# Score matmuls in four row groups of 32 instead of two of 64, with banks always filled by three and re-planned costs

## The chip, the cores and the metric

One core of one Trainium2 chip. The metric is device time in microseconds (us) of one execution, lower is better. Engines: PE is TensorE, ACT is ScalarE, DVE is VectorE. Times below are medians of several executions.

## The reference, cut to what matters

Two layers, each a multi-query attention block and then a linear-attention block, on x of 2048 x 512. In attention 32 heads of size 16 share one K and one V.

```python
q = (x @ wq)            # 2048 x 32 heads x 16
k = x @ wk              # 2048 x 16, shared by all heads
v = x @ wv
scores = einsum("bhqd,bkd->bhqk", q, k) * 16 ** -0.5
p = softmax(scores)     # 2 layers x 32 heads x 2048 x 2048 exponentials
o = einsum("bhqk,bkd->bhqd", p, v)
```

Cut into tiles of 128 keys x 512 queries, there are 4096 score tiles in the two layers. Every one needs a score matmul, an exponential of 128 x 512 values, and a matmul with V ("PV").

## The kernel before

A scheduler inside the kernel simulates the engines with planned costs and fixes, at build time, in which order each engine gets its instructions. On the chip only semaphores decide when they start. So a planned cost is never executed, but it shapes the order.

Score tiles go two ways. ACT takes two or three PSUM banks at a time ("a fill") and computes exp on 1024 or 1536 columns. DVE takes tiles through bank 6 and computes exp by arithmetic, in pairs ("DVE score tiles"). The kernel uses eight PSUM banks: 0 to 2 and 3 to 5 are ACT's two sets, 6 serves DVE's scores and all other work (projections, transposes), 7 collects PV.

```python
    RG = 64                                  # rows of the array per score matmul
    NRG, NM = P // RG, RG // DH              # 2 row groups, 4 masked copies of K
    FILL, FILLW, FILLN = 0.6, 1.7, 512       # aim for PE's streaming share
    SHARE = True                             # bank 5 may be lent to other work
    ...
    def tdv(n, c=1.04): return 0.065 + n * c * 1e-3    # planned cost on DVE
    def tac(n):         return 0.09 + n * 0.833e-3     # planned cost on ACT
    ...
        # one fill: a score matmul per bank, row group i of head i
        def smm(self, e, ps_, b0):
            for k, p in enumerate(ps_):
                ...
                r = slice(i * RG, (i + 1) * RG)
                x = e.matmul(bank(b0 + k), lhsT=Kr[r, m, kt * P:(kt + 1) * P],
                             rhs=QT[r, ...], start=True, stop=True)
    ...
            for s in (0, 1):                 # the two sets of banks
                w = 3
                if s == 1 and SHARE and (not banks.free[5] or (not banks.free[6] and self.waiting())):
                    w = 2                    # second set without bank 5
    ...
    def idle(now):                           # PE has nothing to do: zero matmul into bank 7
        if not sc.order[PE] or streaming(now) > FILL * FILLW:
            return
        ...
        o = add(PE, ..., lambda e: e.matmul(bank(7, FILLN), lhsT=zer[:], rhs=maskx[:].bitcast(BF16)[:, 0:FILLN], ...), name="dummy")
```

A head's 16 rows are picked from the row group by a copy of K in which the other rows are zero: RG / 16 copies.

The softmax here doesn't subtract the row's maximum and nothing guards it: scores larger than these inputs give would overflow.

## Time and profile before

| | before |
|---|---|
| time (three executions) | 1849.07 us (1846.9 to 1851.51) |
| exps on ACT | 1039 of 1536 columns, 227 of 1024 |
| DVE score tiles | 523 |
| zero matmuls | 594 |

From the profile's page: the busy line (busy us, share of the span, instructions), the chain that ended last, and four groups (line, engine, operation, out<-in, shapes, count, busy us, mean ns of one, idle time just before them and what ended it).

```profile
PE 1754.5 (95%) x11002; PEld 515.1 (28%) x11002; DVE 1658.7 (90%) x2966; ACT 1739.9 (94%) x1529; POOL 34.2 (2%) x46
...
PE 44%; DVE 43%; ACT 11%; issue 1%; POOL 1%; DMA 0%; SPq 0%
...
L775 ACT ACTIVATE PTA<-ps_all 128x1536 bf16<-128x1536 f32 (+1 forms) x1268 | 1640.6, 1398 | 59.4 <-PE ps_all L635 52.1
L635 PE MATMUL ps_all<-QT,Kr 64*128 64x512 bf16 x4096 | 835.1, 383 | 42.0 <-DVE xT L829 16.0
...
L829 DVE TENSOR_SCALAR xT<-ps_all 128x512 int32<-128x512 f32 x523 | 358.8, 686 | 48.9 <-PE ps_all L635 45.7
...
L897 PE MATMUL ps_all<-maskx,zer 128*128 128x512 bf16 x594 | 205.0, 387 | 0.0
```

Three engines are at 90% or more. L775 is ACT's exp, L635 the score matmul, L897 the zero matmul, L829 DVE's first step on a score tile. The timeline of PE (start us, us, what) shows two fills:

```profile
441.57 0.40 PE L671 MATMUL ps_all<-PTA,Vaug 128*32 128x512 bf16 x3
441.90 0.39 PE L897 MATMUL ps_all<-maskx,zer 128*128 128x512 bf16 x1
442.22 0.60 PE L635 MATMUL ps_all<-QT,Kr 64*128 64x512 bf16 x3
442.75 0.40 PE L671 MATMUL ps_all<-PTA,Vaug 128*32 128x512 bf16 x3
443.08 0.39 PE L897 MATMUL ps_all<-maskx,zer 128*128 128x512 bf16 x1
443.40 0.60 PE L635 MATMUL ps_all<-QT,Kr 64*128 64x512 bf16 x3
```

Three scores take 0.60 us: two start together in different row groups, the third a pass (0.21 us) later. From a score group's start to the next PV it is 0.53 us, from PV to a zero matmul and from there to the scores 0.32 to 0.33 each.

Two stretches with many projections (busy us and instruction count of each engine; ACT is the fourth), and ACT's longest wait (total us, times, longest):

```profile
450.00:500.00 50.00, 49.75 (x312) 14.74 (x308) 43.19 (x84) 46.28 (x42) 2.60 (x4) 1.00 0.00 1
650.00:700.00 50.00, 48.72 (x291) 13.71 (x290) 46.12 (x88) 46.11 (x39) 3.54 (x4) 1.00 0.00 1
```

```profile
ACT PTA L775 <- PE ps_all L635: 52.1, 127, 1.5
```

**An account of ACT.** "Busy" hides short delays. Where exps run without a visible wait in the timeline, one of 1536 columns starts 1.33 to 1.36 us after the other; 1.336 is taken as ACT's own time. A 1024-column one is taken as 0.92 us (an estimate: intervals of 0.90 and, with hidden waits, 1.03 us were seen), a 512-column one as 0.48, a phi exp as 0.49. The span is cut into the two long stretches of attention and the "ends" (the ramp, the change of layers, the tail). Own time is count times cost. What the ends take beyond own time is "ends"; what attention takes beyond it is ACT's **loss**. Before, these are 1629 own, 117 ends and 99 loss, together the span of 1845.4 us.

### The profile page before, as it was taken

What the parts mean: (1) busy time and instruction counts of PE and PEld (TensorE: products, weight loads), DVE (VectorE), ACT (ScalarE), POOL (GpSimd) and SP (SyncE); (2) the same over time, 40 slices, a digit from 0 to 9 for tenths busy, and PEclk for the clock granted to TensorE, in tenths of its full rate; (3) what the DMA queues carried; (4) which work ended last, traced back from release to release, by engine and by line L of the source; (5) the groups of instructions that cost most, each with busy time, mean ns of one, the idle gap of its engine ahead of it and who ended that gap; (6) DMA issues with size and microseconds to landing.
All of it is one profiled execution on the core that took longest, in us unless ns stands there. A gap on an engine that the chain in (4) does not pass through costs nothing.

```text
span 1845.4 us, 26741 instructions
## 1 busy us (share of the span) xinstructions
PE 1754.5 (95%) x11002; PEld 515.1 (28%) x11002; DVE 1658.7 (90%) x2966; ACT 1739.9 (94%) x1529; POOL 34.2 (2%) x46
## 2 busy tenths in 40 slices
PE   7999999999999999999899999999999999999998
PEld 3222222222222222223342222222223222232224
DVE  7999988999889997998689999899997999989985
ACT  7999999999999999999699999999999999999996
POOL 0000000000000000000000000000000000000000
PEclk9999999999999999999999999999999999999999
DMA  3000000000000000000000000000000000000001
GB/s 115 1 1 1 1 1 1 1 1 1 1 1 1 1 1 1 1 1 1 1 1 1 1 1 1 1 1 1 1 1 1 1 1 1 1 1 1 1 1 46
DMA packets 7722, 9.08 MB, mean 5 GB/s; under 512 B 1456, under 2 KB 7088, under 8 KB 7600
## 3 DMA queue, kind: packets, MB, share of 16 engines
q1 hardware_dynamic: 7600, 7.37, 1.2%
q8 instruction: 86, 1.41, 0.3%
q14 instruction: 36, 0.29, 0.1%
HBM read 5.28 MB, written 2.10 MB: 4 GB/s over the span
## 4 chain that ended last, share of the span: by engine, by line
PE 44%; DVE 43%; ACT 11%; issue 1%; POOL 1%; DMA 0%; SPq 0%
PE ps_all L635 17%; PE ps_all L671 13%; ACT PTA L775 10%; DVE xT L829 9%; DVE PTD L851 8%; PE ps_all L496 7%; DVE xs L850 5%; DVE xs L847 5%; DVE xu L846 4%; DVE xu L849 3%; DVE xs L848 2%; PE ps_all L897 2%; PE ps_all L692 1%; DVE Eo L683 1%; DVE stats L461 1%
## 5 line engine op out<-in xcount | busy, mean ns | idle before, releaser
L775 ACT ACTIVATE PTA<-ps_all 128x1536 bf16<-128x1536 f32 (+1 forms) x1268 | 1640.6, 1398 | 59.4 <-PE ps_all L635 52.1
L635 PE MATMUL ps_all<-QT,Kr 64*128 64x512 bf16 x4096 | 835.1, 383 | 42.0 <-DVE xT L829 16.0
L671 PE MATMUL ps_all<-PTA,Vaug 128*32 128x512 bf16 x3573 | 539.3, 389 | 3.4 <-DVE Eo L683 2.8
L829 DVE TENSOR_SCALAR xT<-ps_all 128x512 int32<-128x512 f32 x523 | 358.8, 686 | 48.9 <-PE ps_all L635 45.7
L851 DVE SCALAR_TENSOR_TENSOR PTD<-xT,xs 128x1024 uint16<-128x1024 int32 (+1 forms) x262 | 318.4, 1215 | 1.4
L635 PEld LDWEIGHTS ps_all<-QT,Kr 64*128 64x128 bf16 x4096 | 175.2, 93 | 500.9 <-ACT PTA L775 198.2
L671 PEld LDWEIGHTS ps_all<-PTA,Vaug 128*32 128x32 bf16 x3573 | 129.5, 93 | 463.4 <-issue 451.5
L897 PE MATMUL ps_all<-maskx,zer 128*128 128x512 bf16 x594 | 205.0, 387 | 0.0
L846 DVE TENSOR_SCALAR xu<-xT 128x1024 f16<-128x1024 uint16 (+1 forms) x262 | 180.2, 688 | 3.0
L850 DVE TENSOR_TENSOR xs<-xs,xu 128x1024 f16<-128x1024 f16 (+1 forms) x262 | 179.0, 684 | 3.0
L847 DVE TENSOR_TENSOR xs<-xu 128x1024 f16<-128x1024 f16 (+1 forms) x262 | 178.7, 682 | 2.0
L671 PE MATMUL ps_all<-PTD,Vaug 128*32 128x512 bf16 x523 | 144.3, 385 | 16.4 <-DVE Eo L683 12.9
L848 DVE TENSOR_SCALAR xs<-xs 128x1024 f16<-128x1024 f16 (+1 forms) x262 | 109.6, 418 | 2.1
L849 DVE TENSOR_SCALAR xu<-xu 128x1024 f16<-128x1024 f16 (+1 forms) x262 | 109.5, 418 | 0.0
L897 PEld LDWEIGHTS ps_all<-maskx,zer 128*128 128x128 bf16 x594 | 48.7, 96 | 105.0 <-issue 98.3
L496 PE MATMUL ps_all<-wqkv_sb,xnT 128*128 128x512 bf16 x256 | 70.9, 383 | 3.3 <-DVE xnT L485 1.1
L469 POOL TENSOR_TENSOR rstd<-veps,mhalf 128x1 f32<-128x1 f32 x30 | 30.7, 1025 | 1731.1 <-DVE veps L467 1723.3
L940 DVE TENSOR_SCALAR e_buf<-e_buf 128x512 f32<-128x512 f32 x64 | 26.9, 422 | 32.8 <-ACT e_buf L939 32.5
L671 PEld LDWEIGHTS ps_all<-PTD,Vaug 128*32 128x32 bf16 x523 | 32.3, 94 | 65.3 <-DVE Eo L683 27.7
L692 PE MATMUL ps_all<-identf,Eo 128*128 128x128 f32 x256 | 42.0, 287 | 5.6 <-DVE Eo L683 4.0
L939 ACT ACTIVATE e_buf<-ps_all 128x512 f32<-128x512 f32 x64 | 39.0, 610 | 8.3 <-PE ps_all L496 6.1
L461 DVE BATCH_NORM_STATS2 stats<-x_sb 128x6 f32<-128x512 bf16 x64 | 43.2, 683 | 3.3 <-DMA x_sb<-in_A_x_dram 2.6
(87 smaller groups left out, 841.6 us busy)
## 6 DMA issues: line engine op xcount, KB each, us to landing
out_dram<-x_sb SPq DMA_DIRECT2D x16, 128.0 KB, 1.7
x_sb<-in_A_x_dram SPq DMA_DIRECT2D x3, 512.0 KB, 6.7
wqkv_sb<-in_B_wqkv_dram SPq DMA_DIRECT2D x1, 1536.0 KB, 11.6
x_sb<-in_A_x_dram SPq DMA_DIRECT2D x2, 256.0 KB, 3.1
wq_sb<-in_A_wq_dram SPq DMA_DIRECT2D x1, 512.0 KB, 4.6
wo_sb<-in_A_wo_dram SPq DMA_DIRECT2D x1, 512.0 KB, 8.5
wo_sb<-in_B_wo_dram SPq DMA_DIRECT2D x1, 512.0 KB, 10.9
wk_sb<-in_A_wk_dram SPq DMA_DIRECT2D x1, 16.0 KB, 2.6
```

Source lines behind the costliest of these rows:

```text
L496: i = e.matmul(bank(h.idx, n), lhsT=l, rhs=r, start=(c + k == 0), stop=(c + k == len(mms) - 1))
L635: x = e.matmul(bank(b0 + k), lhsT=Kr[r, m, kt * P:(kt + 1) * P], rhs=QT[r, self.units[u][0] % 2, gs, q0:q0 + n], start=True, stop=True)
L671: return e.matmul(ps[32 * c:32 * c + 32, 7 * 512:8 * 512], lhsT=Vaug[:, kt, :], rhs=src, start=opened[0], stop=opened[1], skip_group_check ...
L775: oe = add(AC, tac(m * 512), lambda e: e.activation(PTA[:, hp.idx, 0:m * 512], bank(3 * s, m * 512), ACTF.Exp, scale=SCALE), deps=[o] + pr ...
L829: o = add(DV, tdv(512), lambda e: e.tensor_scalar(out=xT[:, hx.idx, i * 512:(i + 1) * 512], in0=bank(6), scalar1=SCALE * LOG2E * 65536.0, ...
L846: o = add(DV, tdv(w, 0.52), lambda e: e.tensor_scalar(out=u_, in0=lo, scalar1=1.0 / 65536, scalar2=-0.5, op0=ALU.mult, op1=ALU.add), deps= ...
L847: o1 = add(DV, tdv(w, 0.52), lambda e: e.tensor_tensor(out=s_, in0=u_, in1=u_, op=ALU.mult), deps=[o] + c["prev"], name="xsq", **kw)
L848: o2 = add(DV, tdv(w, 0.26), lambda e: e.tensor_scalar(out=s_, in0=s_, scalar1=XK, scalar2=-XW, op0=ALU.mult, op1=ALU.add), deps=[o1], nam ...
L849: o3 = add(DV, tdv(w, 0.26), lambda e: e.tensor_scalar(out=u_, in0=u_, scalar1=1.0, scalar2=XL, op0=ALU.mult, op1=ALU.add), deps=[o1], nam ...
L850: o4 = add(DV, tdv(w, 0.52), lambda e: e.tensor_tensor(out=s_, in0=s_, in1=u_, op=ALU.mult), deps=[o2, o3], name="xc", **kw)
L851: o5 = add(DV, tdv(w), lambda e: e.scalar_tensor_tensor(out=PTD[:, hp.idx, 0:w].bitcast(U16), in0=xT[:, k, 0:w], scalar=2.0 ** -9, in1=s_, ...
L897: o = add(PE, 0.03 + FILLN * 0.41e-3, lambda e: e.matmul(bank(7, FILLN), lhsT=zer[:], rhs=maskx[:].bitcast(BF16)[:, 0:FILLN], start=not ow ...
```

## The change

The intent: K copies masked within 32 rows instead of 64 let four score matmuls run side by side, so three take one pass; two copies of K are enough; ACT's two sets always take three banks; the memory set free holds a third buffer for DVE; and the scheduler's planned costs are brought nearer to measured ones.

```diff
-    RG = 64
+    RG = 32
-    SHARE = True
+    SHARE = False
-    NPA, NPD, NDX = 5, 6, 2
+    NPA, NPD, NDX = 5, 6, 3
     def tdv(n, c=1.04):
-        return 0.065 + n * c * 1e-3
+        return 0.068 + n * c * 1e-3
     def tac(n):
-        return 0.09 + n * 0.833e-3
+        return 0.0525 + n * 0.8325e-3
 ... (seven more planned costs of small DVE operations and of K's copies, e.g. 0.4 -> 0.333 for a copy) ...
-            o = add(PE, 0.05 + 0.14 * m, f, ..., name="sA")
+            o = add(PE, 0.2 + 0.014 * m if RG == 32 else 0.05 + 0.14 * m, f, ..., name="sA")
-            st = {"pv": 0.071, "sA": 0.4, "dummy": 0.2}.get(...)
+            st = {"pv": 0.071, "sA": 0.2 if RG == 32 else 0.4, "dummy": 0.2}.get(...)
```

The last line makes the filler count a score group as half the streaming it was, so it adds more zero matmuls.

## The prediction

> **What bounds it now.** The page gives PE 95%, ACT 94% and DVE 90% busy, PE clock 1.0 in every slice. A PE record covers a matmul's latency (383 ns for 512 columns, while concurrent ones start together), so PE's 95% says little. ACT is the floor: its exps are 1,640.6 us of the 1,845.4 us span. In the timeline, runs of nothing but 1536-column exps start every 1.335 to 1.36 us (1.336 used below), and a 1024-column exp costs about 0.92 us: 1039 x 1.336 + 227 x 0.92 = 1,597 us. Ramp, the change of layers and the tail (stretches 0-46, 890-952 and 1804-1845) cost about 122 us net of exps, the 64 phi exps in attention about 35 us. About 90 us are left in attention in which ACT is not running at its own rate. The waits view says for what: 52 us, 127 times, for score matmuls (L635); the rest are short delays that "busy" hides. The losses gather where projections also use PE: 50 us windows at 450, 650, 850 have ACT 40 to 46 us busy, quiet ones 49.
>
> **Why PE is late there.** With two row groups a fill of three scores takes two passes (0.60 us, third start 0.21 later). In the timeline scores-to-PV is 0.54 us, PV-to-scores 0.33: 0.87 us a fill before DVE tiles, zero matmuls and projections, against about 1.27 us of ACT. A change of matmul kind costs about 0.11 us beyond the 0.21 us pass; the Trainium skill, "TensorEngine Tiling (Array Packing)", Key Properties, says changing the tiling mode drains TensorE, which fits.
>
> **What the change does.** Counted from the built programs:
> - Three scores of different row groups should run as one pass: about 0.39 us, scores-to-PV 0.33, so 0.66 us a fill, 0.21 us less, on about 1,204 fills: 250 us of PE time. The skill, "TensorE: Matmul & The Clock Gate", Part 3, measured 3.07x for four row tiles.
> - Zero matmuls 594 -> 1234. At 0.21 to 0.33 us each that takes back 135 to 210 us, in the stretches where the schedule thinks PE idle, not beside projections.
> - Exps: 1039 of 1536 and 227 of 1024 become 1204 and 3. Bank 5 is no longer lent, so bank 6 serves DVE scores and all else in attention; DVE score tiles fall 523 -> 478, ACT gets 45 tiles more. ACT exps: 1204 x 1.336 + 3 = 1,611 us, **14 us more**.
> - DVE loses about 130 us (45 evictions at 0.69, 22 chains at 4.1 us, 19 K copies): about 83% busy.
> - K copies 64 -> 32 (0.47 us each), mostly in the ramps: 5 us off the path.
>
> **Sum.** ACT's own work 1,597 -> 1,611; phi 35; ramps and ends 122 -> 117; loss in attention 90 -> about 43, because PE has 0.3 us more per fill where projections run. 1,611+35+117+43 = **1806 us**, 2.3% less. 80%: 1784 to 1838. Faster by over 2%: 0.55; within 2%: 0.41; slower: 0.04.
>
> **What would show it.** Score groups of 0.39 us instead of 0.60; ACT's waits for L635 under 30 us; exps busy about 1,650 us; ACT 96% busy; DVE near 83%; clock still 1.0; PE still near 90% busy (zero matmuls).
>
> **What would make it wrong.** 32-row matmuls counting less as activity, so that the clock drops (slower); row groups not overlapping, or a dearer mode change; bank 6 alone delaying projections, so a backlog at each layer's end (the 850-950 stretch longer); zero matmuls placed where the real PE is not idle, keeping ACT's waits; or more recovered than half (1770s).

## The result, and the profile after

| | before | after |
|---|---|---|
| time, median (range) | 1849.94 (1846.9 to 1851.51) | 1780.67 (1778.53 to 1782.28) |
| ratio | | 0.9627, 95% interval 0.9609 to 0.9644 |
| exps of 1536 / 1024 | 1039 / 227 | 1204 / 3 |
| DVE score tiles | 523 | 478 |
| zero matmuls | 594 | 1234 |
| own + ends + loss | 1629 + 117 + 99 | 1643 + 112 + 23 |

A ratio is the mean time of one kernel's executions over that of the other's in the same rounds, so it is not quite the ratio of the medians. Executions over 1.5% slower than the fastest of the same kernel are left out of the means. The change gains 3.7%. That is more than predicted, and 3 us under the low end of the range.

The same lines of the page, after:

```profile
PE 1683.0 (95%) x11642; PEld 533.4 (30%) x11642; DVE 1554.0 (87%) x2767; ACT 1728.1 (97%) x1452; POOL 31.3 (2%) x46
...
ACT 62%; PE 19%; DVE 17%; issue 1%; DMA 0%; POOL 0%; SPq 0%
...
L775 ACT ACTIVATE PTA<-ps_all 128x1536 bf16<-128x1536 f32 x1207 | 1644.0, 1569 | 7.7 <-PE ps_all L635 6.3
L635 PE MATMUL ps_all<-QT,Kr 32*128 32x512 bf16 x4096 | 611.3, 385 | 39.8 <-ACT PTA L775 14.8
...
L897 PE MATMUL ps_all<-maskx,zer 128*128 128x512 bf16 x1234 | 401.0, 386 | 0.0
L829 DVE TENSOR_SCALAR xT<-ps_all 128x512 int32<-128x512 f32 x478 | 327.4, 685 | 80.8 <-PE ps_all L635 78.9
```

The chain that ended last has turned from PE and DVE to ACT. Score matmuls fell from 835 to 611 us busy, 224 us less; zero matmuls rose from 205 to 401, 196 us more. So the zero matmuls took back nearly all that the row groups freed, and PE is 95% busy as before. PE's timeline:

```profile
400.22 0.39 PE L635 MATMUL ps_all<-QT,Kr 32*128 32x512 bf16 x3
400.55 0.40 PE L671 MATMUL ps_all<-PTA,Vaug 128*32 128x512 bf16 x3
400.87 0.82 PE L897 MATMUL ps_all<-maskx,zer 128*128 128x512 bf16 x3
401.63 0.39 PE L635 MATMUL ps_all<-QT,Kr 32*128 32x512 bf16 x3
401.95 0.40 PE L671 MATMUL ps_all<-PTA,Vaug 128*32 128x512 bf16 x3
402.28 0.39 PE L897 MATMUL ps_all<-maskx,zer 128*128 128x512 bf16 x1
```

Three scores now take 0.39 us, all starting within 0.01 us, and PV starts 0.33 us after them. This agrees with the Trainium skill, "TensorE: Matmul & The Clock Gate", Part 3, where row tiles run concurrently. The projection stretches, and ACT's wait for scores:

```profile
450.00:500.00 50.00, 46.98 (x316) 14.09 (x313) 41.17 (x74) 49.78 (x40) 1.91 (x2) 1.00 0.00 1
650.00:700.00 50.00, 48.10 (x325) 14.72 (x325) 44.09 (x81) 50.00 (x40) 2.20 (x3) 1.00 0.00 1
```

```profile
ACT PTA L775 <- PE ps_all L635: 6.3, 23, 1.1
```

ACT is busy for all but 0.2 us of these 100. The zero matmuls alone (L897) in the same stretches, before:

```profile
450.00:500.00 50.00, 1.15 (x3) 0.29 (x3) 1.00 0.00 1
650.00:700.00 50.00, 3.80 (x12) 0.82 (x11) 1.00 0.00 1
```

and after:

```profile
450.00:500.00 50.00, 9.78 (x30) 2.25 (x30) 1.00 0.00 1
650.00:700.00 50.00, 9.94 (x30) 2.41 (x30) 1.00 0.00 1
```

So beside projections, too, zero matmuls came in: they take 15 us more of these 100, while the scores take 9 us less (43.7 and 34.6). The stretches do not hold quite the same work: their projections (L496) are 21.0 us before and 15.4 after. ACT's loss fell by 76 us where 47 were predicted. The experiments ask which part of the change did that.

### The profile page after: what moved, and what is told of

The parts are those of the page before. It is cut to its first block, busy times and chain, and to the rows that moved or that the text cites. A ratio compares the mean times of both kernels' runs of the same rounds, so it can differ in the third digit from the quotient of the medians.

```text
span 1777.9 us, 27691 instructions
## 1 busy us (share of the span) xinstructions
PE 1683.0 (95%) x11642; PEld 533.4 (30%) x11642; DVE 1554.0 (87%) x2767; ACT 1728.1 (97%) x1452; POOL 31.3 (2%) x46
## 4 chain that ended last, share of the span: by engine, by line
ACT 62%; PE 19%; DVE 17%; issue 1%; DMA 0%; POOL 0%; SPq 0%
ACT PTA L775 60%; PE ps_all L635 6%; PE ps_all L671 5%; PE ps_all L897 3%; DVE xT L829 3%; DVE PTD L851 3%; PE ps_all L496 2%; ACT e_buf L939 1%; DVE xs L847 1%; DVE xu L846 1%; DVE xs L850 1%; DVE stats L461 1%; PE ps_all L1060 1%; DVE xs L848 1%; DVE xu L849 1%
## 5 line engine op out<-in xcount | busy, mean ns | idle before, releaser
L775 ACT ACTIVATE PTA<-ps_all 128x1536 bf16<-128x1536 f32 x1207 | 1644.0, 1569 | 7.7 <-PE ps_all L635 6.3
L635 PE MATMUL ps_all<-QT,Kr 32*128 32x512 bf16 x4096 | 611.3, 385 | 39.8 <-ACT PTA L775 14.8
L897 PE MATMUL ps_all<-maskx,zer 128*128 128x512 bf16 x1234 | 401.0, 386 | 0.0
L635 PEld LDWEIGHTS ps_all<-QT,Kr 32*128 32x128 bf16 x4096 | 147.2, 91 | 486.3 <-ACT PTA L775 188.1
L851 DVE SCALAR_TENSOR_TENSOR PTD<-xT,xs 128x1024 uint16<-128x1024 int32 x239 | 290.3, 1215 | 1.8
L846 DVE TENSOR_SCALAR xu<-xT 128x1024 f16<-128x1024 uint16 x239 | 164.3, 687 | 3.7
L847 DVE TENSOR_TENSOR xs<-xu 128x1024 f16<-128x1024 f16 x239 | 163.5, 684 | 2.9
L850 DVE TENSOR_TENSOR xs<-xs,xu 128x1024 f16<-128x1024 f16 x239 | 163.0, 682 | 2.4
L897 PEld LDWEIGHTS ps_all<-maskx,zer 128*128 128x128 bf16 x1234 | 93.9, 97 | 196.5 <-issue 179.4
L848 DVE TENSOR_SCALAR xs<-xs 128x1024 f16<-128x1024 f16 x239 | 98.9, 414 | 1.7
L849 DVE TENSOR_SCALAR xu<-xu 128x1024 f16<-128x1024 f16 x239 | 99.2, 415 | 0.0
L496 PE MATMUL ps_all<-wqkv_sb,xnT 128*128 128x512 bf16 x256 | 68.7, 382 | 1.5 <-DVE xT L829 0.9
L940 DVE TENSOR_SCALAR e_buf<-e_buf 128x512 f32<-128x512 f32 x64 | 27.1, 423 | 45.4 <-ACT e_buf L939 45.2
```

The source lines that it names most:

```text
L496: i = e.matmul(bank(h.idx, n), lhsT=l, rhs=r, start=(c + k == 0), stop=(c + k == len(mms) - 1))
L775: oe = add(AC, tac(m * 512), lambda e: e.activation(PTA[:, hp.idx, 0:m * 512], bank(3 * s, m * 512), ACTF.Exp, scale=SCALE), deps=[o] + pr ...
L846: o = add(DV, tdv(w, 0.52), lambda e: e.tensor_scalar(out=u_, in0=lo, scalar1=1.0 / 65536, scalar2=-0.5, op0=ALU.mult, op1=ALU.add), deps= ...
L847: o1 = add(DV, tdv(w, 0.52), lambda e: e.tensor_tensor(out=s_, in0=u_, in1=u_, op=ALU.mult), deps=[o] + c["prev"], name="xsq", **kw)
L848: o2 = add(DV, tdv(w, 0.26), lambda e: e.tensor_scalar(out=s_, in0=s_, scalar1=XK, scalar2=-XW, op0=ALU.mult, op1=ALU.add), deps=[o1], nam ...
L849: o3 = add(DV, tdv(w, 0.26), lambda e: e.tensor_scalar(out=u_, in0=u_, scalar1=1.0, scalar2=XL, op0=ALU.mult, op1=ALU.add), deps=[o1], nam ...
```

## The experiments

Three parts can be taken alone: **R**, four row groups (with their planned cost and zero matmuls); **B**, banks always by three; **C**, the new planned costs. Three theories stood at the start. P: the saved PE pass (R) frees ACT, as predicted. B: filling by three does. M: the re-planned costs do. Each run is correct unless said, and was timed in three rounds beside the kernel before, whose median was 1849 to 1850 us throughout. "Loss" is that of the account above, from the run's trace.

### The three parts, alone and together

**e1_rg64**: R undone. The third buffer had to go too: four copies of K leave no room for it.

```diff
-    RG = 32
+    RG = 64
-    NPA, NPD, NDX = 5, 6, 3
+    NPA, NPD, NDX = 5, 6, 2
```

> The changed kernel with two row groups again (RG = 64; banks by three and the new costs stay; only two DVE buffers, since four copies of K leave no room for the third). Its schedule has 523 zero matmuls, 1208 exps of 1536, 464 DVE score tiles. Theory P (the saved TensorE pass per fill is what freed ScalarE): most of the gain is lost, 1825 to 1855 us, score groups 0.60 us, ScalarE's waits for score matmuls back above 30 us. Theory B (filling banks always by three is what helped): stays below 1800 us. Theory M (the recalibrated costs of the scheduler): stays below 1800 us.

Measured 1802.51 us (ratio 0.9755), loss 29 us, ACT's waits for scores 9 us. This is between the theories' numbers (P: 1825 or more; B and M: below 1800). Most of the gain stays without four row groups.

**e2_share**: B undone.

```diff
-    SHARE = False
+    SHARE = True
```

> The changed kernel with bank 5 lent out again (SHARE = True): 943 exps of 1536, 362 of 1024, 542 DVE score tiles. Exps' own work falls to about 943 x 1.336 + 362 x 0.92 = 1593 us, 18 us less than the changed kernel's. Theory P: ScalarE's loss in attention stays near 23 us, so about 1765 us. Theory B: pairs leave PE only 0.92 us for the next fill, the loss returns (above 60 us), 1810 to 1845 us. Theory M: about 1765 us.

Measured 1795.05 to 1804.07 us in three executions (ratio 0.9722). A fourth, the profiled one, took 4859.79 us: its clock fell during one 20 us window and never came back. In these windows the granted clock is the third number from the right, 1.00, 0.80 and 0.16:

```profile
800.00:820.00 20.00, 18.04 (x122) 5.58 (x123) 19.65 (x35) 20.00 (x16) 0.00 (x0) 1.00 0.00 1
820.00:840.00 20.00, 18.41 (x99) 4.49 (x101) 17.24 (x28) 17.96 (x16) 0.00 (x0) 0.80 0.00 0
840.00:860.00 20.00, 20.00 (x36) 2.79 (x35) 5.87 (x13) 5.74 (x5) 0.00 (x0) 0.16 0.00 1
```

It is left out of every comparison; its cause stays open. Up to 820 us this trace ran at full clock but for 3.4 us, and there its loss is 27 us, against 47 in the kernel before, 41 in `e7_before_rg32`, 38 in `e9_before_newcosts` and 9 in the changed kernel. In the first three of these four the whole loss is 2.1 to 2.2 times that, so about 60 us here (estimate). Lending bank 5 costs about 19 us although ACT has 18 us less of its own to do. Theories P and M expected about 1765 us and missed; B expected 1810 or more, which was too much.

**e3_oldcosts**: C undone (all planned costs as before, third buffer kept).

```diff
-        return 0.0525 + n * 0.8325e-3
+        return 0.09 + n * 0.833e-3
 ... and the other costs likewise ...
```

> The changed kernel with the scheduler's old durations for DVE and ACT (the order of instructions changes, no instruction does): 1329 zero matmuls, 1200 exps of 1536, 492 DVE score tiles. Theory M: loses 20 us or more, above 1800 us. Theories P and B: within 10 us of the changed kernel (1771 to 1791 us), somewhat less work for ScalarE (14 tiles, 6 us).

Measured 1807.8 us (ratio 0.9772), loss 55 us. No instruction differs in kind, only the order and the share of each engine, and 27 us are gone.

**e6_ndx2**: the third buffer undone.

```diff
-    NPA, NPD, NDX = 5, 6, 3
+    NPA, NPD, NDX = 5, 6, 2
```

> The changed kernel with two DVE buffers instead of three (468 DVE score tiles, 1208 exps of 1536). The third buffer should be worth little: ten tiles more on ScalarE are 4.5 us, so 1780 to 1792 us.

Measured 1782.11 us, loss 27 us in a trace whose clock had a dip (0.993). As expected, it is worth about nothing, so it is not in the way when the parts are compared.

**e7_before_rg32**: R alone on the kernel before.

```diff
-    RG = 64
+    RG = 32
-            o = add(PE, 0.05 + 0.14 * m, f, ...
+            o = add(PE, 0.2 + 0.014 * m, f, ...
-            st = {"pv": 0.071, "sA": 0.4, ...
+            st = {"pv": 0.071, "sA": 0.2, ...
```

> The kernel before with four row groups alone (RG = 32 and the scheduler's figures for it; bank 5 still lent, old costs, two buffers): 1270 zero matmuls, 1054 exps of 1536, 201 of 1024, 531 DVE score tiles; exps' own work 1054 x 1.336 + 201 x 0.92 = 1593 us, 4 us less than before. Theory P: nearly the whole gain, 1765 to 1795 us. Theory B: most of the loss stays, above 1815 us.

Measured 1828.75 us (ratio 0.9886), loss 90 us. ACT still waits for scores:

```profile
ACT PTA L775 <- PE ps_all L635: 45.4, 124, 1.4
```

The passes are saved here (scores 637 us busy instead of 835), and the waits of 52 us become 45. **Theory P falls as the main cause of the smaller loss.**

**e8_before_by3**: B alone on the kernel before.

```diff
-    SHARE = True
+    SHARE = False
```

> The kernel before with banks always by three alone (bank 5 not lent; two row groups, old costs): 1206 exps of 1536, 2 of 1024, 472 DVE score tiles; exps' own work 1613 us, 16 us more than before. Theory P: PE is still late, so 1845 to 1870 us. Theory B: PE has 1.34 us per fill instead of 0.92 for every other one, the loss falls, 1790 to 1820 us.

Measured 1815.61 us (ratio 0.9819), loss 53 us, with PE as slow per fill as ever:

```profile
ACT PTA L775 <- PE ps_all L635: 20.8, 63, 1.3
```

**e9_before_newcosts**: C alone on the kernel before (two buffers).

```diff
-        return 0.09 + n * 0.833e-3
+        return 0.0525 + n * 0.8325e-3
 ... and the other costs likewise ...
```

> The kernel before with the recalibrated costs alone (two row groups, bank 5 lent, two buffers): 1044 exps of 1536, 225 of 1024, 514 DVE score tiles. Completes the eight combinations of the three parts. If the parts add up as they do elsewhere (costs took 20 to 29 us off wherever they were tried), 1820 to 1832 us, ScalarE's loss in attention near 75 us. If the costs only pay with banks by three: above 1840 us.

Measured 1829.72 us (ratio 0.9894), loss 78 us. The eight combinations:

| parts | run | time us | own | ends | loss |
|---|---|---|---|---|---|
| none | before | 1849.07 | 1629 | 117 | 99 |
| R | e7 | 1828.75 | 1625 | 111 | 90 |
| B | e8 | 1815.61 | 1645 | 118 | 53 |
| C | e9 | 1829.72 | 1633 | 118 | 78 |
| R, B (3 buffers) | e3 | 1807.8 | 1636 | 110 | 55 |
| R, C (3 buffers) | e2 | 1799.59 | 1625 | - | about 60 (estimate) |
| B, C (2 buffers) | e1 | 1802.51 | 1649 | 121 | 29 |
| R, B, C (2 buffers) | e6 | 1782.11 | 1647 | 114 | 27 |
| R, B, C (3 buffers) | after | 1780.67 | 1643 | 112 | 23 |

The columns add up to the traced execution, not to the median. How to read it: with two row groups B takes 46 us off the loss without C (99 to 53) and 49 with it (78 to 29); with four row groups it takes 35 (90 to 55) and about 37. It pays 11 to 18 us of own time, as ACT gets more tiles. C takes 21 to 32 off (24 and 32 with B). R takes 9 off alone, about 18 with C (the estimate for e2), none with B (53 to 55), and 2 to 6 with both. In the mean of the four settings B takes about 42 of the 76 us, C 27 and R 7.

In time the three are much closer, since B pays for its gain: B is worth 19 to 34 us (mean 25), C 13 to 29 (mean 22), R 8 to 30 (mean 20). R's 20 us come as much from the ends, 6 to 9 us shorter (K's copies are 32 instead of 64, which probably is why), and from own time, 2 to 9 us less, as from the loss.

### Why banks by three help

**e11_pairs**: the changed kernel, but the second set always takes two banks, and bank 5 lies unused.

```diff
-                if s == 1 and SHARE and (not banks.free[5] or (not banks.free[6] and self.waiting())):
+                if s == 1 and not self.ramp:
                     w = 2
```

> The changed kernel, but the second set of banks always takes two tiles and bank 5 stays unused (nothing else borrows it): 728 exps of 1536, 710 of 1024; exps' own work 1626 us, 15 us more. Theory B1 (the short exp of a pair leaves PE only 0.92 us for the next fill, so ScalarE waits): the loss in attention goes from 23 to above 50 us, 1825 us or more. Theory B2 (it was the borrower of bank 5, a projection or a transpose, that held the second set up, not the size): the loss stays below 30 us, 1795 to 1805 us.

Two executions took 1833.1 and 1833.94 us at clock 1.0; two more, 1861 us at clock 0.981, are counted as slow. The ratio is 0.9915, the loss 62 us:

```profile
ACT PTA L775 <- PE ps_all L635: 26.7, 84, 1.0
```

So B1 holds: the size of the fill alone, without a borrower, brings the loss back. PE must refill the one set while ACT works on the other. That gives it 1.34 us beside a fill of three, and 0.92 us beside a pair. Pairs also mean more fills (1438 instead of 1207) and so more changes of matmul kind on PE; this run does not part the two.

The trace of the kernel before says where the lateness sits. There the next exp starts, in the mean, 0.27 us later than a 1024-column exp's own 0.904 us allows (225 of them, 61 us), but only 0.04 us later than a 1536-column one's own 1.331 us (1020 of them, 44 us). In the changed kernel 1185 fills of three leave 0.025 us each. The borrower (B2) is not ruled out as a smaller part: a pair is followed by 0.094 us of lateness in this run, where bank 5 lies unused, and by 0.136 us in `e2_share` up to 820 us, where it is lent.

### Why the freed PE time takes so little off the loss

**e4_nofill**: the changed kernel without zero matmuls.

```diff
-    FILL, FILLW, FILLN = 0.6, 1.7, 512
+    FILL, FILLW, FILLN = 0.0, 1.7, 512
```

> The changed kernel without zero matmuls (5 are left of 1234), exps as before the edit (1201 of 1536). If they hold the clock up, the mean granted clock falls well under 1.0 and score groups and PV take longer: slower, 1800 us or more. If the clock stays at 1.0 they only cost PE time: 1765 to 1781 us.

Measured 1917.97 us (ratio 1.0372), mean clock 0.789, loss 158 us. In windows of 5 us the clock (again third from the right) stands at one half or at full:

```profile
200.00:205.00 5.00, 4.67 (x21) 0.72 (x19) 3.98 (x7) 4.16 (x4) 0.00 (x0) 0.50 0.00 0
...
210.00:215.00 5.00, 3.74 (x30) 1.32 (x31) 5.00 (x11) 5.00 (x5) 0.00 (x0) 1.00 0.00 0
```

The zero matmuls are needed. They are not free, though: they are the price of four row groups, as the next run shows.

**e10_rg64_nofill**: two row groups (e1_rg64), without zero matmuls (`RG = 64`, `NDX = 2`, `FILL = 0.0`).

> Two row groups, banks by three, new costs (e1_rg64) without zero matmuls (5 of 523 left). Without them the four-row-group kernel ran at a clock of 0.79. If a longer stay of PE in the scores (0.60 us a fill, not 0.39) does the work of the zero matmuls, the clock here is much nearer 1.0, above 0.93, and the time 1800 to 1830 us. If the clock depends on the zero matmuls alike: about 0.8 and 1880 us or more.

Measured 1805.3 us (ratio 0.9767), as e1_rg64 with its zero matmuls (1802.51):

```profile
core 0: 1802.2 us, clock 0.988
```

With two row groups the clock all but holds by itself. With four it needs zero matmuls, and they use up the passes saved.

**e5_rep**: the changed kernel, the third score of each fill issued twice, nothing else touched. (The edit adds a line, so line numbers are one higher.)

```diff
-                x = e.matmul(bank(b0 + k), ...)
+                for rep in range(2 if k == len(ps_) - 1 and len(ps_) == 3 else 1):
+                    x = e.matmul(bank(b0 + k), ...)
```

> The changed kernel, same schedule instruction by instruction, but the third score of every fill of three is issued twice (same row group, same bank, overwritten with the same values): one TensorE pass more per fill, 0.21 us, as with two row groups. Theory P: ScalarE's waits for score matmuls come back, its loss in attention rises from 23 us to 60 us or more, 1815 to 1850 us. Theories B and M: the schedule is unchanged, within 10 us of 1781 us.

Measured 1935.09 us (ratio 1.047), far above the 1815 to 1850 that P expected, and B and M, with 1771 to 1791, missed by more. The loss is 174 us, at clock 1.0:

```profile
ACT PTA L776 <- PE ps_all L636: 95.1, 277, 1.2
```

This is no proof of theory P, for the kernel with two row groups needs the same pass and runs in 1802 us. It shows that, with 1234 zero matmuls fixed in it, this order has no room for a pass more per fill. From the steps in the timelines (estimate): scores to PV 0.53, PV to a zero matmul and on to the next scores 0.33 each, make 1.19 us, and DVE's tiles, 0.4 per fill, come on top, against 1.336 us of ACT. The two-row-group kernel has the pass but only 523 zero matmuls; the changed kernel has 1234 but not the pass. That it is the zero matmuls that leave no room is not shown by a run: the one without them, next, ran at a low clock.

**e13_rep_nofill**: the repeated score without zero matmuls. Does a pass of 32 rows do the zero matmuls' work?

```diff
-    FILL, FILLW, FILLN = 0.6, 1.7, 512
+    FILL, FILLW, FILLN = 0.0, 1.7, 512
 ... and the repeated score of e5_rep ...
```

> The changed kernel without zero matmuls (5 left), but with the third score of each fill issued twice, as in e5_rep. If the pass that four row groups save is the very activity that the zero matmuls have to replace, the clock comes back from 0.79 to above 0.95 and the time from 1918 to 1785 to 1820 us. If the clock asks for matmuls over all 128 rows (as the zero matmuls are), it stays below 0.85 and the time above 1900 us.

Measured 2137.0 us (ratio 1.1558). The clock per fortieth of the span, in tenths:

```profile
PEclk9856578756699859976786775696558998698658
```

The mean of the traced run is 0.746, no better than without the repeat (0.789).

**e17_zero32**: the zero matmuls contract over 32 rows; same number and places.

```diff
-  lhsT=zer[:], rhs=maskx[:].bitcast(BF16)[:, 0:FILLN]
+  lhsT=zer[0:32, :], rhs=maskx[0:32, :].bitcast(BF16)[:, 0:FILLN]
```

> The changed kernel with the zero matmuls contracted over 32 rows instead of 128 (same number, 1234, same places, same 512 columns). If the clock counts how long TensorE streams, it stays near 1.0 and the time near 1781 us. If it counts rows in use, the zero matmuls lose three quarters of their worth: clock below 0.9 and 1840 us or more.

Measured 1908.6 us (ratio 1.0329), clock 0.869 in the trace, loss 147 us:

```profile
L897 PE MATMUL ps_all<-maskx,zer 32*128 32x512 bf16 x1234 | 441.4, 422 | 0.0
```

Equal in count and columns, but with a quarter of the rows, they hold the clock far less well. With e13 this says that rows in use count, not only time. One rival is that a 32-row zero matmul overlaps a score in another row group, so that PE streams for less time here. The traces speak against it.

As an estimate, count a 512-column matmul as 0.216 us of streaming at full clock, the shortest usual step between zero matmuls in a row, and twice that at half clock, and look at windows of 3.41 us, the step in which the clock records change. At full clock PE then streams 69% of the time both here and in the changed kernel; weighted with the rows in use, as a share of 128, it is 50% here and 60% there. In the eight traces that have all their zero matmuls, each of 150 drops to half clock followed a window with a weighted share under 0.40, while the unweighted share before a drop was up to 0.76. 113 other windows that low were not followed by a drop. And e13_rep_nofill and e10_rg64_nofill both stream 67% of the time at full clock, but weighted 48% and 58%, with mean clocks of 0.746 and 0.988.

**e12_fill50**: fewer zero matmuls (798).

```diff
-    FILL, FILLW, FILLN = 0.6, 1.7, 512
+    FILL, FILLW, FILLN = 0.5, 1.7, 512
```

> The changed kernel with the aim for PE's streaming share at 0.5 instead of 0.6: 798 zero matmuls instead of 1234, exps the same. If 0.6 is more than the clock needs, PE is freer: 1770 to 1780 us at a clock of 1.0. If it needs it: a clock below 0.97 and 1790 us or more.

Measured 1782.34 us, clock 0.988 in the trace, loss 21 us. Neither theory's numbers came: a third of the zero matmuls can go, the clock falls slightly, and the time does not move.

### Which planned cost, and why

**e14_oldact**: only ACT's planned cost undone.

```diff
-        return 0.0525 + n * 0.8325e-3
+        return 0.09 + n * 0.833e-3
```

> The changed kernel with only ScalarE's old cost in the scheduler (1.370 us for an exp of 1536, where the trace shows 1.335 to 1.345; now 1.331): 1199 exps of 1536, 494 DVE score tiles. Undoing all costs took it to 1808 us. If ScalarE's cost is what matters (the order then expects ScalarE 3% later than it comes), 1800 to 1808 us; else within 8 us of 1781 us.

Measured 1808.24 us (ratio 0.9774), loss 59 us: all that C is worth here (e3_oldcosts was 1807.8).

**e15_olddve**: only the DVE costs and those of K's copies undone, that is, every cost but ACT's.

> The changed kernel with only the old VectorE costs (and the old ones of the K copies): 1205 exps of 1536, 479 DVE score tiles. The complement of e14: if ScalarE's cost is what matters, within 8 us of 1781 us; if the VectorE ones do, 1795 us or more.

Measured 1778.46 us (1776.34 to 1783.32), loss 29 us in the slowest execution, the traced one (clock 0.992): no different in time from the changed kernel.

**e18_actfast**: ACT's cost planned too low.

```diff
-        return 0.0525 + n * 0.8325e-3
+        return 0.0125 + n * 0.8325e-3
```

> The changed kernel with ScalarE's cost in the scheduler set 0.04 us too low (1.291 us for an exp of 1536; 1.336 measured, 1.331 in the change, 1.370 before): 1208 exps of 1536, 4 of 1024, 463 DVE score tiles, 1122 zero matmuls. Theory of pace (the fixed order lets ScalarE run no faster than the pace it was planned for, since TensorE and VectorE work is interleaved at that pace; planning too slow costs, too fast does not): the loss in attention stays below 25 us, 1780 to 1792 us with 6 us more own work. Theory of exactness (any error costs): 1800 us or more.

Measured 1781.71 us, loss 17 us. Dividing the time in attention without phi and smaller exps by the number of 1536-column exps gives the pace of ACT (for e14: 835.9 + 832.7 - 31 us over 1182):

| planned for one exp | pace measured | loss |
|---|---|---|
| 1.370 (e14) | 1.386 | 59 |
| 1.331 (after) | 1.356 | 23 |
| 1.291 (e18) | 1.350 | 17 |

ACT is held to the pace it was planned for and not beyond its own speed. Planned slow, it is slow; planned fast, it only waits for nothing. The likely reason is that a fixed order puts a set amount of PE and DVE work between two fills; this fits the table, but no run shows which wait passes it on. The number of zero matmuls changes with the plan, too (1122 in e18), but e12_fill50, with 436 fewer than the changed kernel, has nearly its loss.

### A try for a faster version

**e16_moredve**: ACT is the floor now, so give DVE more. The rule that hands bank 6 to other work after each DVE score is removed, with FILL 0.5.

```diff
-            if self.dlast and self.waiting():
-                return False
-    FILL, FILLW, FILLN = 0.6, 1.7, 512
+    FILL, FILLW, FILLN = 0.5, 1.7, 512
```

> The changed kernel with the zero-matmul aim 0.5 and without the rule that lets other work have bank 6 after each DVE score: 1180 exps of 1536, 552 DVE score tiles. A try for a faster version: 24 exps fewer are 32 us less for ScalarE, VectorE gets 74 tiles x 2.7 us = 200 us more, to 98% of the span, which will not fit without waits. 1755 us if nothing else waits; 1790 us or more if projections starve for bank 6 and the change of layers grows.

Measured 1850.43 us (ratio 1.0). The run has 65.8 us of ACT waits for scores, the longest 7.5 us, and 45.2 us for projections, at a clock of 0.964. Its 74 more DVE tiles cost more than they save, the waits and the lower clock included. No version here beats the changed kernel clearly.

## Why the prediction was wrong

1. **ACT is the floor** (1,597 us of exps): right. Exps' busy time became 1,644.0 us, ACT 97% busy, and the chain turned to ACT.
2. **ACT's own exps 14 us more, ends 5 us less**: right, 1629 to 1643 and 117 to 112.
3. **Score groups in one pass, 0.39 us, 0.33 to PV**: right. **Zero matmuls take back 135 to 210 us**: right, 196. But "not beside projections" was wrong: in the two projection stretches they went from 15 to 60.
4. **"loss in attention 90 -> about 43, because PE has 0.3 us more per fill where projections run"**: this step failed, in size and in cause. Measured 99 before and 23 after: 76 us off, not 47, and in the sum itself 23 for 43 is 20 of the 25 us missed. The freed PE time was not the main cause: alone, four row groups took 9 us off the loss (e7), and on top of the rest 2 to 6 (e1 against e6 and after). Where projections run, zero matmuls took more (15 us in the two stretches) than the scores saved (9 us). Filling by three took 46 to 49 with two row groups (e8, e1 against e9) and 35 with four (e3 against e7), since fills by two hold ACT up (e11; in the kernel before, 0.27 us after each pair), most likely because a pair leaves PE only 0.92 us for the next fill. ACT's planned cost took the rest (e14, e15). The prediction counted filling by three as a cost alone (14 us more for ACT) and did not mention the planned costs. That the sign was right and the time no more than 25 us off is in part luck: the loss fell mainly for reasons that the prediction did not have.
5. **The list of dangers**: the clock danger was real (0.789 without zero matmuls) and the zero matmuls met it. Bank 6 did not make the ends longer. "More recovered than half (1770s)" was named as a way to be wrong, and that is what came (76 of 99 us; 1780.67 us).
6. **DVE near 83%**: 87% of a shorter span. Its busy time fell by 105 us, not 130.

## What to carry to other kernels

When an engine works through two buffers by turns, the smaller buffer sets how long the producer has for the other: equal, full-sized buffers can be worth more than a faster producer. In this statically ordered kernel, a planned cost 2.5% too high for the bottleneck engine (1.370 for 1.336 us) was a speed limit, and one 0.04 us too low cost nothing; calibrate that one first. When a change frees time on one engine, look for what takes it back before counting it: here the zero matmuls that keep the clock up took nearly all of it, and four row groups still gained 8 to 30 us, much of it elsewhere.

## What the Trainium skill lacked or had wrong

- "TensorE: Matmul & The Clock Gate", Part 1, says that the clock follows how busy PE has been and gives no weight to rows in use. Here it does depend on them: 1234 zero matmuls on 128 rows held 0.998, the same on 32 rows 0.869, none 0.789.
- The same page, "Why this matters for your kernels", asks for no idle gaps over about 3 us. That was not enough: without zero matmuls, PE was never idle for longer than 1.4 us in attention, and the clock still went to 0.50 in stretches. In kind this is no news, for the page's "A second HAM failure mode" tells of frequent short idles that make the clock swing; what no page has is how much activity is enough (here no drop after a window with a row-weighted share of 0.40 or more, an estimate, see e17_zero32). That it stands at half or full agrees with the page's table of two states.
- That matmuls with zero weights count as activity is not stated by the page; they held the clock at 0.998. Its remark on zero data is about the current limiter alone.
- The page warns of a clock stuck at a quarter for over 50 us. One execution here stayed at 0.16 from 835 us to its end at 4857.6 us, about 4.0 ms, lower and longer.
- "TensorEngine Tiling (Array Packing)", Key Properties, says that a change of tiling mode drains TensorE, but has no cost. Score to PV takes 0.32 to 0.33 us where a pass is 0.21, so about 0.11 us more; that this is the drain is not shown apart.
